# Linear attention into a SiLU layer on one core: units 12 to 15 join the seven-product scheme, half of the scores are masked in SBUF, and the last product ends in three pieces

## The chip, the cores and the metric

The kernel runs on one core of a Trainium2 chip. The metric is device time in microseconds (us) for one execution. The kernel before takes 203.23 us, the median of three runs (203.1, 203.23 and 203.87).

## What is computed

The reference first runs a blocked linear attention and then a two-layer network on its output (cut to what matters):

```python
# q, k, v: (4, 8, 768, 64) float32; lam: (8,); blocks of 64 positions
intra = (qb @ kb.T) * Dmask            # Dmask[i, j] = lam ** (i - j) where i >= j, else 0
out_b = intra @ vb + (qb * lam_pow) @ kv_state
kv_state = lam_block * kv_state + (kb * rev_pow).T @ vb
...
x = out.transpose(0, 2, 1, 3).reshape(3072, 512)
h = x @ w_in                           # 512 -> 2048
g = h * sigmoid(h)                     # SiLU
return g @ w_out                       # 2048 -> 512, float32
```

The decay `lam ** (i - j)` is split into a factor on v and a factor on the result, so the scores themselves are only multiplied by a triangle of ones and zeros.

## The kernel before, in words

**Units, pairs, groups.** The 3072 rows are cut into 24 units of 128 rows. Attention works on pairs of units (12 pairs, three per batch entry). The first product (x @ w_in, here called P1) works on groups: four groups of two units for units 0 to 7, then groups of four for units 8 to 23. The second product (g @ w_out, P2) works on one unit (`product2`, L970) for units 0 to 11 and on four units (`product2_of_four`, L1061) from unit 12 on (`SEVENS = 12`).

**Attention of a pair.** `prepare` (L523) loads k, q and v in float32 (L429), casts k and q to bf16 (tile `kq`), scales v (`vd`) and gets the transposes `kqT`: on TensorE for the first four pairs, by one DMA transpose on SyncE's queue (L590) from pair 4 on. From pair 3 on, `burst` (L600) issues on TensorE, as one block of 64-row matmuls, the scores (L667) and states (L656) of the new pair and the outputs (L623, L630) of the pair before it. `attention` (L728) then reads the four score banks of a pair (two halves g, two row halves h) in PSUM, multiplies each by the triangle `tri` and writes bf16 into `st`: four VectorE operations of 128x512 a pair, the line that the profile gives as L411. The next burst reads `st`. The outputs are multiplied by the decay into `xt` (also L411), the input of P1.

**P1.** `product1` (L919) fills a PSUM bank with matmuls (L933) and ScalarE writes SiLU of it into `g` (L949). In a group of four units one tile takes four 128x512 matmuls, 64 in all for the group. `product1_of_four` (L1212), used for units 16 to 19 and 20 to 23 (`FIRST_SEVENS = (16, 20)`), forms the same result as seven products of sums in place of eight: 28 matmuls of 128x256 (L1252) for each of four quarters j, 112 a group. It needs sums of quarters of w_in (`wsum`, eight half tiles, `sums_of_w_in`, L1197), four differences of x (`xsum`), and for each j three copies of a bank (`to u` into another bank, `u2` and `u3` into SBUF) and two additions (`h22`, `h12`, L1015), with four SiLUs (L1268).

**P2.** `product2_of_four` forms seven products, too (L1124): numbers 3, 4, 5, 1, 2, 7, 6 of the table `SEVEN`, and for the last four units 3, 4, 2, 1, 5, 7, 6. It accumulates in PSUM on top of copies: product 3 goes into bank A, A is copied into bank P (`to P`), product 4 is added on P, the negative of P is copied into B (`to B`), and so on; a product cannot start before the copy that it adds on. It needs sums of w_out (`bsum`, L1015 on VectorE or GpSimd, or a DMA copy L1048 and an accumulating DMA L1051 for the three in `BMOVED`) and sums of g (`asum`, likewise, or by the DMAs L1105 and L1111 for units 12 to 19). For the last four units the last product (6) goes unit by unit into two banks, is copied out by VectorE (first unit, L406) and ScalarE (second unit, L404) and stored by two queues (L962).

**Order.** Nothing runs in the order in which the code is read. Every step is a task with a key (its due time), the engines that may do it and their costs, its dependencies and its buffers. `Planner.order` (L107) replays all tasks by those numbers and writes down the order for every engine; the instructions are then issued in that order, and each engine keeps it. `SHIFT` moves keys by tag and `HOME` fixes an engine for a tag. `LATE` and `TLATE` are the extra us that the plan allows for the landing of a load and of a transpose from pair 4 on (both 4.0). TensorE's idle stretches before 19 us in the plan are filled with matmuls on ones (L1319).

Of the kernel before, what the change touches and what calls it, by code (L numbers as in the profile page):

```python
# [39 lines left out]
def names_of(tag):  # L40


    if not isinstance(tag, tuple):
        return tag, None, None
    kind, n = tag[:2]
    if kind in ("cast", "scale", "burst", "mask", "y", "xe", "xf", "xt"):
        whole = "pair", n
    elif kind in ("first", "silu", "x", "to u", "u2", "u3", "h12", "h22"):
        whole = "group", n
    elif kind in ("seven", "a", "a copy", "to P", "to B", "to R", "on R", "m3", "c11", "c12", "c21", "c22"):  # L50
        whole = "four", n
    else:
        whole = None
    return tag, tag[:2] if len(tag) > 2 else None, whole


class Planner:
# [7 lines left out]

    SHIFT = {('cast', 11, 1, 0): -0.5, ('cast', 5, 0, 1): 2, ('cast', 7, 1, 0): 7, ('cast o', 2, 0): -5, ('first', 2, 3): 1.5,
             ('first', 2, 5): 3, ('first', 2, 7): 1.75, ('first', 5): 3.25, ('first', 5, 10): 6.25, ('first', 5, 12): 6,
             ('first', 5, 13): 10.25, ('first', 5, 15): 7, ('first', 5, 8): 3, ('first', 6): 7, ('first', 6, 0, 5): -3.75,
             ('first', 6, 1, 2): -0.25, ('first', 6, 1, 5): 5.5, ('first', 6, 2, 1): 1.25, ('first', 6, 2, 2): 4,
             ('first', 6, 2, 3): 7, ('first', 6, 3, 4): 0.25, ('first', 6, 3, 7): 5.5, ('first', 7, 0, 7): 1.5,  # L70
             ('first', 7, 1, 2): -6.75, ('four', 20): 2.5, ('group', 5): -6, ('group', 6): 0.5, ('inter', 2, 0): 9.75,
             ('load w', 3, 1): -1.5, ('pair', 10): -7.25, ('pair', 4): 0.25, ('pair', 5): -6, ('pair', 7): -9, ('pair', 9): -8.5,
             ('result', 1): -0.5, ('scale', 3, 0): -1, ('scale', 8): -5.5, ('second', 0): 2.25, ('seven', 12, 1): 10.5,
             ('seven', 16): 13.25, ('seven', 16, 6): 5.25, ('seven', 20): 14, ('store', 9): -2, ('to u', 7, 1): 0.5,
             ('turn', 1, 0, 0): -4.75, ('turned', 1, 0, 1): 5, ('turned', 2): 8.25, ('xe', 0, 0, 1): 4.5, ('xe', 3, 0, 0): 1.5,
             ('xe', 9, 0, 0): -3, ('xf', 6): -1.5, ('y', 10, 0, 0): -3.5, ('y', 6): -2.5, ('y', 8, 0, 0): -2}
    HOME = {('a', 20, 2, 1): 'POOL', ('b', 4, 0): 'POOL', ('cast', 10, 1, 0): 'DVE', ('cast', 11, 0, 0): 'ACT',
            ('cast', 11, 0, 1): 'DVE', ('cast', 11, 1, 0): 'ACT', ('cast', 11, 1, 1): 'DVE', ('cast', 3, 0, 1): 'ACT',
            ('cast', 4, 0, 0): 'ACT', ('cast', 4, 0, 1): 'DVE', ('cast', 5, 0, 0): 'POOL', ('cast', 5, 1, 0): 'ACT',
            ('cast', 7, 1, 0): 'DVE', ('cast', 8, 0, 0): 'POOL', ('cast', 8, 1, 0): 'POOL', ('cast', 9, 0, 0): 'POOL',  # L80
            ('cast', 9, 1, 0): 'POOL', ('cast o', 2, 0): 'DVE', ('cast o', 3, 1): 'DVE', ('cast o', 3, 3): 'DVE',
            ('cast w', 1, 3): 'POOL', ('result', 1): 'ACT', ('scale', 10, 0): 'POOL', ('to P', 12): 'ACT', ('to u', 7, 1): 'ACT',
            ('turned', 0, 1, 0): 'ACT', ('turned', 2, 0, 0): 'DVE', ('turned', 2, 0, 1): 'ACT', ('u3', 6, 0): 'ACT',
            ('u3', 7, 2): 'DVE', ('w', 3, 0): 'POOL', ('x', 6, 4): 'POOL', ('x', 7, 2): 'POOL', ('xe', 4, 0, 0): 'DVE',
            ('xe', 6, 0, 0): 'POOL'}
    FIRST, LAST, AHEAD = {"SP": 1.15, "ACT": 1.15, "POOL": 1.0}, 1.0, 0.75
# [196 lines left out]
def kernel(  # L283
# [130 lines left out]
    raw = {}  # L414
    LATE, TLATE = 4.0, 4.0

# [56 lines left out]

    groups = [[0, 1], [2, 3], [4, 5], [6, 7], ] + [list(range(4 * n, 4 * n + 4)) for n in range(2, NU // 4)]
    group_of = {u: (gi, i) for gi, us in enumerate(groups) for i, u in enumerate(us)}
# [252 lines left out]
    def attention(n):  # L728
# [332 lines left out]
    def product2_of_four(us):  # L1061
# [15 lines left out]
        def product(i, m, bank, opens, after=(), split=False):  # L1077
# [39 lines left out]
            prev, done = None, []  # L1117
            for p in ([(0,), (1,)] if split else [(0, 1)]):
                for ko in range(8):
                    buf, ready, lhs = left[ko]  # L1120

                    def mm(e, p=p, ko=ko, lhs=lhs):
                        for u in p:
                            nc.tensor.matmul(part(bank, u), lhsT=lhs(u), rhs=b_of(ko), stop=ko == 7, skip_group_check=True,  # L1124
                                             start=opens and not ko and not u)

                    prev = add((key + (ko + 8 * p[0] / len(p)) / 28, 2), {"PE": len(p) * (256 / 2400 + 0.0025)}, mm,
                               deps=[ready, bdeps[ko], prev] + list(after), kind="p2", tag=("seven", us[0], m),
# [51 lines left out]
        if not final:  # L1180
# [3 lines left out]
            return  # L1184
        for u, on, to in ((0, {"DVE": 0.42}, "SP"), (1, {"ACT": 0.39}, "ACT")):
            o = Buf("rawh")
            c22 = add(at(7), on, lambda e, u=u, o=o: copy(e, osb_of(o, 1)[:, 0], part(R, u)), deps=[m6[u]], bufs=[R[u], o], tag=("c22", tag, u))
            stored((at(7.3)[0], 7), halves_of[1], slice(128 * us[2 + u], 128 * us[2 + u] + 128), o, c22, on=to)

# [153 lines left out]
    at = 0.0  # L1343
# [40 lines left out]
```

## Time and profile before

| | before |
|---|---|
| runs | 203.1, 203.23, 203.87 us (median 203.23) |
| the profiled execution | 203.53 us, of which its span is 201.6 us and 1.93 us lie around it |
| mean granted TensorE clock | 0.999 |
| P1, units 8 to 15: matmuls 128x512 (L933) | 128 |
| P1 by seven products: matmuls 128x256 (L1252) | 224 |
| VectorE busy, 100 to 120 us, its fullest stretch of 20 us | 17.25 of 20 us |
| HBM read and written | 27.27 and 6.29 MB |

How to read it: the span runs from the first to the last instruction of the profiled execution. The page names engines PE (TensorE), PEld (its weight loads), DVE (VectorE), ACT (ScalarE), POOL (GpSimd) and SP (SyncE); a q behind the name is the queue that issues DMAs. In a group of instructions, "out<-in xcount | busy, mean ns | idle before <-releaser" gives what is written from what, how many, the total in us, the mean duration of one in ns, and how long the engine had been idle just ahead of them and for whom. The chain of work that ended last lists, in order of time, start in us, duration in us and what ran. A matmul's own duration reaches beyond the start of the next one, so the pace of a row of matmuls is read from that chain (duration over count), not from the mean.

### The profile page before, as it was taken

Reading aid. Unit: us, or ns where it says so; the run is one execution under the profiler, and the core shown is the slowest. Engines: PE = TensorE matmul, PEld = TensorE weight load, DVE = VectorE, ACT = ScalarE, POOL = GpSimd, SP = SyncE. Lnnn points to the kernel's source line nnn. Section 1 sums busy time; section 2 is a strip of 40 time slices with the busy share of each in tenths; the row PEclk is TensorE's granted clock in tenths of the full one; section 3 lists DMA queues with packets and bytes.
Section 4 is the critical chain, followed back from the end, with each engine's and each line's share of the span. In section 5 each row is a group of like instructions: output and inputs, shape, how many; then the busy total and the mean of one; then the engine's idle time right before and its main releaser. Section 6 shows DMA issues by size and latency. Waiting matters only on the chain.

```text
span 201.6 us, 5956 instructions
## 1 busy us (share of the span) xinstructions
PE 195.3 (97%) x2526; PEld 138.2 (69%) x2526; DVE 142.3 (71%) x235; ACT 122.3 (61%) x189; POOL 68.2 (34%) x81
## 2 busy tenths in 40 slices
PE   6998999999999999999999999999999999999993
PEld 2776788867766554544545455458888888888882
DVE  3798848686972649599596987983854758837282
ACT  3776798838786533178777515756775688862210
POOL 4024510524602020589053305418862433004000
PEclk9999999999999999999999999999999999999999
DMA  4999999999999999989999999938998969002223
GB/s 109 331 343 367 368 366 345 379 295 378 287 210 291 249 336 337 319 216 278 268 223 324 222 259 215 183 105 181 188 176 245 193 226 196 9 3 104 81 99 135
DMA packets 77898, 47.57 MB, mean 236 GB/s; under 512 B 18544, under 2 KB 70768, under 8 KB 77872
## 3 DMA queue, kind: packets, MB, share of 16 engines
q1 hardware_dynamic: 64976, 35.79, 64.4%
q0 software_dynamic: 8576, 6.03, 20.8%
q10 hardware_dynamic: 4320, 5.38, 7.4%
q8 instruction: 20, 0.33, 0.6%
q14 instruction: 6, 0.05, 0.1%
HBM read 27.27 MB, written 6.29 MB: 166 GB/s over the span
## 4 chain that ended last, share of the span: by engine, by line
PE 89%; SPq 5%; DMA 3%; ACT 1%; issue 0%
PE banks L933 28%; PE banks L975 21%; PE banks L1124 18%; PE banks L1252 12%; SPq L429 4%; DMA raw_w<-in_moe_w_in_dram 3%; PE banks L667 2%; PE banks L623 2%; PE banks L630 1%; PE banks L656 1%; PE banks L575 1%; SPq L448 1%; PE banks L896 1%; PE banks L846 1%; PE banks L877 0%
## 5 line engine op out<-in xcount | busy, mean ns | idle before, releaser
L933 PE MATMUL banks<-xt,w_in_bf 128*128 128x256 bf16 (+1 forms) x384 | 64.2, 308 | 0.7 <-ACT w_in_bf L404 0.4
L949 ACT ACTIVATE g<-banks 128x512 bf16<-128x512 f32 x64 | 46.3, 744 | 18.5 <-PE banks L933 15.7
L933 PEld LDWEIGHTS <-w_in_bf 128*128 128x128 bf16 x384 | 36.7, 98 | 20.4 <-ACT w_in_bf L404 0.6
L975 PE MATMUL banks<-w_out_bf,g 128*128 128x512 bf16 x192 | 47.7, 379 | 0.0
L411 DVE TENSOR_TENSOR st<-banks,tri 128x512 bf16<-128x512 f32 (+1 forms) x42 | 29.9, 759 | 5.8 <-PE banks L667 4.2
L975 PEld LDWEIGHTS <-g 128*128 128x128 bf16 x192 | 18.2, 98 | 19.8
L411 DVE TENSOR_TENSOR xt<-banks,lam_xe 128x512 bf16<-128x512 f32 x24 | 16.0, 687 | 13.3 <-PE banks L623 9.7
L404 ACT ACTIVATE osb<-banks 128x512 f32<-128x512 f32 (+1 forms) x15 | 8.7, 581 | 24.1 <-PE banks L975 18.4
L408 POOL CAST kq<-raw 64x512 bf16<-64x512 f32 (+1 forms) x16 | 15.0, 961 | 18.1 <-DMA raw<-in_q_dram 16.1
L404 ACT ACTIVATE kq<-raw 64x1024 bf16<-64x1024 f32 (+2 forms) x21 | 18.1, 883 | 2.5 <-DMA raw<-in_v_dram 1.5
L1124 PE MATMUL banks<-bsum,g 128*128 128x256 bf16 x160 | 19.4, 273 | 0.0
L1124 PEld LDWEIGHTS <-asum 128*128 128x128 bf16 x176 | 17.2, 98 | 2.0
L1124 PEld LDWEIGHTS <-g 128*128 128x128 bf16 x160 | 15.7, 98 | 1.8
L1111 POOL DMA_DIRECT2D asum<-g x8 | 9.9, 1281 | 17.8 <-DMA asum<-g 11.0
L411 DVE TENSOR_TENSOR vd<-raw,lam_v 128x1024 bf16<-128x1024 f32 (+1 forms) x12 | 13.6, 1130 | 3.0 <-DMA raw<-in_v_dram 2.9
L1268 ACT ACTIVATE g<-banks 128x512 bf16<-128x512 f32 x16 | 11.6, 741 | 4.5 <-PE banks L1252 4.3
L1252 PE MATMUL banks<-xsum,wsum 128*128 128x256 bf16 x96 | 14.2, 273 | 0.0
L1252 PEld LDWEIGHTS <-wsum 128*128 128x128 bf16 x128 | 12.4, 98 | 1.7
L411 POOL TENSOR_TENSOR xf<-y,lam_be 128x256 f32<-128x256 f32 (+1 forms) x6 | 4.9, 811 | 22.9 <-DVE y L787 16.9
L1319 PE MATMUL banks<-ones 128*128 128x128 bf16 (+1 forms) x90 | 10.9, 271 | 1.5 <-DVE ones L355 1.5
L1015 DVE TENSOR_TENSOR tmp<-banks,tmp 128x512 f32<-128x512 f32 x16 | 10.9, 688 | 2.0 <-ACT tmp L404 1.1
L406 DVE CAST kq<-raw 64x512 bf16<-64x512 f32 (+3 forms) x21 | 10.3, 512 | 2.9 <-DMA raw<-in_k_dram 2.5
(96 smaller groups left out, 284.4 us busy)
## 6 DMA issues: line engine op xcount, KB each, us to landing
raw<-in_k_dram SPq DMA_DIRECT2D x11, 512.0 KB, 7.3
raw<-in_q_dram SPq DMA_DIRECT2D x11, 512.0 KB, 6.0
raw<-in_v_dram SPq DMA_DIRECT2D x11, 512.0 KB, 6.7
out_dram<-osb ACTq DMA_DIRECT2D x20, 256.0 KB, 4.4
raw_w<-in_moe_w_in_dram SPq DMA_DIRECT2D x8, 512.0 KB, 7.9
raw_w<-in_moe_w_out_dram SPq DMA_DIRECT2D x8, 512.0 KB, 7.0
asum<-g SPq DMA_DIRECT2D x8, 256.0 KB, 2.6
asum<-g POOLq DMA_DIRECT2D x8, 256.0 KB, 5.3
```

Of the source, the lines that this page charges most:

```text
L404: nc.scalar.activation(o, i, AF.Copy)
L406: nc.vector.tensor_copy(o, i)
L408: nc.gpsimd.tensor_copy(o, i)
L411: (nc.vector if e == "DVE" else nc.gpsimd).tensor_tensor(o, a, b, op=AL.mult)
L933: nc.tensor.matmul(t[:, j, :], lhsT=w_in_bf[:, ko, 128 * m:128 * m + 128], rhs=xt[gi].tile[:, ko, :], start=(ko == 0), stop=(ko == KI - 1))
L949: nc.scalar.activation(t.rearrange("p j (c a r) -> p (j c) r a", c=n // U, r=2), psum_of(bank).rearrange("p (jc r a) -> p jc r a", r=2, a= ...
L975: nc.tensor.matmul(psum_of(bank), lhsT=gs[gi, ko][1](1, 128 * gp, 128)[:, 0], rhs=w_out_bf[:, ko], start=(ko == 0), stop=(ko == KO - 1))
L1015: (nc.vector if e == "DVE" else nc.gpsimd).tensor_tensor(o, x, y, op=op)
L1124: nc.tensor.matmul(part(bank, u), lhsT=lhs(u), rhs=b_of(ko), stop=ko == 7, skip_group_check=True, start=opens and not ko and not u)
L1252: nc.tensor.matmul(two_of(bank)[:, f], lhsT=(wb[0].tile if wb else w_quarter(*wl))[:, ko, fs], rhs=(xsum(xr) if isinstance(xr, int) else x ...
L1268: nc.scalar.activation(t.rearrange("p j (c a r) -> p (j c) r a", c=2, r=2), src().rearrange("p (jc r a) -> p jc r a", r=2, a=64), AF.Silu)
L1319: nc.tensor.matmul((t if b.pool == "bank" else t[:, 0])[:, 0:w], lhsT=ones[:, 0:128], rhs=ones[:, 0:w], start=True, stop=True)
```

## The change

The edit has four parts beside a new set of `SHIFT` and `HOME` entries.

1. `FIRST_SEVENS` gains 12: the group of units 12 to 15 goes through `product1_of_four`. The sums of w_in are now needed for this group as well, so earlier.
2. For pairs 4 to 11 and row half h = 1 (two of the four score banks of a pair), ScalarE copies the bank to `st` as bf16 (tag `take`), and VectorE or GpSimd then multiplies `st` in place by a bf16 triangle `tri_bf` (tag `mask`). The other two banks are masked from PSUM as before.
3. The last product of the last four units is issued as unit 0 with 256 columns, then unit 1 with columns 0 to 127, then unit 1 with columns 128 to 255, each copied and stored by itself.
4. `BMOVED` is emptied: the three sums of w_out that DMAs formed are formed by VectorE or GpSimd. `POOLED` becomes (6, 7): two results are stored by GpSimd's queue. `LATE` and `TLATE` go from 4.0 to 1.0, so the plan lets casts, transposes and bursts stand earlier against TensorE's work.

```diff
-    SHIFT = {('cast', 11, 1, 0): -0.5, ('cast', 5, 0, 1): 2, ...
+    SHIFT = {('a', 12, 6, 1): 10.25, ('a', 20, 6, 1): -9.75, ('b', 6): 7, ...
-    HOME = {('a', 20, 2, 1): 'POOL', ('b', 4, 0): 'POOL', ...
+    HOME = {('a', 12, 1, 1): 'POOL', ('a', 20, 1, 1): 'POOL', ...
...
+    TAKEN = range(4, 12), (1,)
-    BMOVED, POOLED = (1, 7, 6), (6,)
+    BMOVED, POOLED = (), (6, 7)
-    TKEY, SEVENS, LAG, WSKEY, FIRST_SEVENS = 9.0, 12, 5.0, 14.0, (16, 20)
+    TKEY, SEVENS, LAG, WSKEY, FIRST_SEVENS = 9.0, 12, 5.0, 14.0, (12, 16, 20)
...
-    LATE, TLATE = 4.0, 4.0
+    LATE, TLATE = 1.0, 1.0
...
+                    if n in TAKEN[0] and h in TAKEN[1]:
+                        def take(e, st=st, b=b, h=h):
+                            copy(e, tile_of(st, [128, 4, 4 * 64], BF16, "st")[:, 2 * h:2 * h + 2, :], psum_of(b).rearrange("p (m s) -> p m s", m=2))
+
+                        def erase(e, st=st, h=h):
+                            t = st.tile[:, 2 * h:2 * h + 2, :]
+                            mult(e, t, t, tri_bf.rearrange("p r q a -> p (r q a)")[:, None, :].to_broadcast([128, 2, 256]))
+
+                        t = add((s - 0.9, 0, g, h), {"ACT": 0.6}, take, deps=[bursts[1 + g]], bufs=[b, st], tag=("take", n, g, h))
+                        masked.append(add((s - 0.85, 0, g, h), {"DVE": 0.42, "POOL": 1.6}, erase, deps=[t, tri_done], bufs=[st], tag=("mask", n, g, h), lock=True))
+                        continue
...
-            for p in ([(0,), (1,)] if split else [(0, 1)]):
+            for i, (p, cs) in enumerate([((0,), slice(0, 256)), ((1,), slice(0, 128)), ((1,), slice(128, 256))] if split
+                                        else [((0, 1), slice(0, 256))]):
...
-                            nc.tensor.matmul(part(bank, u), lhsT=lhs(u), rhs=b_of(ko), stop=ko == 7, skip_group_check=True,
+                            nc.tensor.matmul(part(bank, u)[:, cs], lhsT=lhs(u), rhs=b_of(ko)[:, cs], stop=ko == 7, skip_group_check=True,
...
-        for u, on, to in ((0, {"DVE": 0.42}, "SP"), (1, {"ACT": 0.39}, "ACT")):
+        for i, (u, cs, on, to) in enumerate(((0, slice(0, 256), {"DVE": 0.42}, "SP"), (1, slice(0, 128), {"DVE": 0.29}, "SP"),
+                                             (1, slice(128, 256), {"ACT": 0.28}, "ACT"))):
...
+    tri_bf = const.tile([128, 2, 2, 64], BF16, name="tri_bf")
+    tri_done = add((-2.9, 0), {"POOL": 0.5}, lambda e: nc.gpsimd.tensor_copy(tri_bf, tri), tag="tri")
```

More of the change, by code (lines that the diff above doesn't have):

```diff
@@ L45, in names_of @@
     kind, n = tag[:2]
-    if kind in ("cast", "scale", "burst", "mask", "y", "xe", "xf", "xt"):
+    if kind in ("cast", "scale", "burst", "mask", "take", "y", "xe", "xf", "xt"):
         whole = "pair", n
@@ L64 @@
     SWITCH = 0.095
[L66 to L85, printed above, removed]
+    SHIFT = {('a', 12, 6, 1): 10.25, ('a', 20, 6, 1): -9.75, ('b', 6): 7, ('cast', 11, 1, 0): -4, ('cast', 11, 1, 1): -0.25,
+             ('cast', 4): 9, ('cast', 4, 0, 0): 0.25, ('cast', 6): -4, ('cast', 8, 1, 0): -4, ('cast', 9, 0, 0): 3.5,
+             ('cast o', 1, 2): 0.25, ('cast o', 2): 5.75, ('first', 2): -11.75, ('first', 2, 1): -5.25, ('first', 2, 6): -11.25,
+             ('first', 3): -0.5, ('first', 3, 5): 2, ('first', 5, 1, 5): 2, ('first', 5, 3, 5): 6.25, ('first', 6): -2.75,
+             ('first', 6, 2, 5): -2.5, ('first', 6, 3, 4): 5.75, ('first', 7): -2.25, ('first', 7, 1, 3): 11.75,
+             ('four', 12): -2.75, ('four', 16): 9.75, ('group', 2): 4.75, ('group', 3): 0.75, ('group', 4): -3.75,
+             ('group', 5): -11.25, ('group', 6): -4, ('group', 7): 0.5, ('load w', 3, 1): -1.5, ('mask', 11, 0, 1): 3,
+             ('mask', 4): 9.5, ('mask', 5): 2.25, ('mask', 5, 1, 0): -1.5, ('mask', 5, 1, 1): -3, ('mask', 6): -3.5,
+             ('mask', 6, 0, 1): 3, ('mask', 7): 0.25, ('mask', 8, 1, 0): -11.25, ('outputs', 1, 1): -9.25, ('outputs', 2, 0): 13.75,
+             ('pair', 10): 9, ('pair', 11): 11.75, ('pair', 4): -7.75, ('pair', 7): -5.75, ('pair', 8): 1.5, ('pair', 9): 1.5,
+             ('scale', 3, 0): -1, ('second', 0): 3.25, ('second', 1): -10.25, ('second', 6): 0.5, ('seven', 12): -4.5,
+             ('seven', 12, 2): 3.75, ('seven', 12, 7): 9.5, ('silu', 5): 3, ('silu', 5, 3, 1, 1): 2.5, ('states', 2, 0): 12.5,
+             ('x', 6): -4, ('x', 6, 1): 5, ('x', 7, 1): 10.5, ('xe', 0, 0, 1): 4.5, ('xe', 3, 0, 0): 1.5, ('xf', 9): 2.75,
+             ('xt', 5): -9, ('y', 10): -2, ('y', 10, 0, 0): -9.25, ('y', 11): 2, ('y', 5): 1.5}
@@ L471 @@
             load_w(n - 100, x[0], int(x[1:]))
-    groups = [[0, 1], [2, 3], [4, 5], [6, 7], ] + [list(range(4 * n, 4 * n + 4)) for n in range(2, NU // 4)]
+    groups = [[0, 1], [2, 3], [4, 5], [6, 7]] + [list(range(4 * n, 4 * n + 4)) for n in range(2, NU // 4)]
     group_of = {u: (gi, i) for gi, us in enumerate(groups) for i, u in enumerate(us)}
@@ L1184, in product2_of_four, with last @@
             return
-        for u, on, to in ((0, {"DVE": 0.42}, "SP"), (1, {"ACT": 0.39}, "ACT")):
+        for i, (u, cs, on, to) in enumerate(((0, slice(0, 256), {"DVE": 0.42}, "SP"), (1, slice(0, 128), {"DVE": 0.29}, "SP"),
+                                             (1, slice(128, 256), {"ACT": 0.28}, "ACT"))):
             o = Buf("rawh")
-            c22 = add(at(7), on, lambda e, u=u, o=o: copy(e, osb_of(o, 1)[:, 0], part(R, u)), deps=[m6[u]], bufs=[R[u], o], tag=("c22", tag, u))
-            stored((at(7.3)[0], 7), halves_of[1], slice(128 * us[2 + u], 128 * us[2 + u] + 128), o, c22, on=to)
+            def last(e, u=u, o=o, cs=cs):
+                copy(e, tile_of(o, [128, 1, cs.stop - cs.start], F32, "osb")[:, 0], part(R, u)[:, cs])
+            c22 = add(at(7), on, last, deps=[m6[i]], bufs=[R[u], o], tag=("c22", tag, i))
+            stored((at(7.3)[0], 7), slice(256 + cs.start, 256 + cs.stop), slice(128 * us[2 + u], 128 * us[2 + u] + 128), o, c22, on=to)
     wsum = {}
```

13 lines of the change are left out of this document (11 added, 2 removed), and 3 rows, old and new, of the table HOME.

## The prediction

> **What bounds the kernel now.** I read the page's busy shares first, then who TensorE waits for, then the chain of work that ended last, in order of time. The first line is the page's busy time, then come the two longest lines of TensorE's waits, apart from one for the ones of the warm-up: what waited, for what, us in total, how often, longest.
>
> ```profile
> PE 195.3 (97%) x2526; PEld 138.2 (69%) x2526; DVE 142.3 (71%) x235; ACT 122.3 (61%) x189; POOL 68.2 (34%) x81
> ```
>
> ```profile
> PE banks L933 <- ACT w_in_bf L404: 0.4, 1, 0.4
> PE banks L933 <- POOL w_in_bf L408: 0.4, 1, 0.4
> ```
>
> A share of 97% could still be slow work, so the chain matters more (start, duration, what ran):
>
> ```profile
> 17.49 0.64 ACT w_in_bf L404
> 18.17 0.83 PE banks L933 x6
> ...
> 27.39 0.45 PE banks L575 x8
> ...
> 69.08 5.18 PE banks L975 x24
> ...
> 159.96 4.15 PE banks L1252 x38
> ...
> 175.90 22.29 PE banks L1124 x204
> 198.20 0.38 ACT osb L404
> ```
>
> From 18.17 to 198.2 us nothing but TensorE carries the chain, and at an even pace: 5.18/24 = 216 ns for 512 columns, 4.15/38 and 22.29/204 = 109 ns for 256, 0.45/8 = 56 ns for 128. So the time is three things: 18.2 us until w_in is cast, 180 us of TensorE's columns, 3.4 us from the last matmul to the end. Fewer columns shorten it one for one; work on other engines costs nothing until TensorE stands still for it. Before has next to no standing still to lose, so every new one adds.
>
> **The change, part by part.** All sums are against the profiled execution, 203.53 us (span 201.6, 1.93 around it); it lies 0.30 above the median 203.23, so I add the sum to the median.
>
> 1. *Units 12 to 15.* Removed: 64 matmuls of 512 columns, 64 x 0.216 = 13.82 us. Added: 112 of 256, 112 x 0.109 = 12.23 us. **-1.59 us**, all of it on the path.
>
> 2. *A new gap ahead of units 16 to 19's second P2 product.* In the changed order the burst of pair 11 no longer follows units 12 to 15's P1 but stands 26 us of TensorE work later, and behind it TensorE has only P2 of units 16 to 19 to do: product 3 (16 matmuls) and then at once product 4, which adds on the copy `to P` of product 3. Nothing stands between. In before each such copy has other matmuls beside it. The price, from these rows (groups of instructions, shapes apart; then the end of the run, in order of time):
>
> ```profile
> L411 DVE TENSOR_TENSOR st<-banks,tri 128x512 bf16<-128x512 f32 x36 | 22.6, 682 | 4.2 <-PE banks L667 4.2
> ...
> L1015 DVE TENSOR_TENSOR wsum<-w_in_bf 128x1024 bf16<-128x1024 bf16 x3 | 5.1, 1737 | 0.0
> ...
> L404 ACT ACTIVATE banks<-banks 128x512 f32<-128x512 f32 x8 | 4.7, 598 | 4.9 <-PE banks L1124 2.9 <-PE banks L1252 2.0
> L1015 POOL TENSOR_TENSOR xsum<-xt,xsum 128x512 bf16<-128x512 bf16 x2 | 4.7, 2346 | 0.0
> ...
> L1015 DVE TENSOR_TENSOR xsum<-xt,xsum 128x512 bf16<-128x512 bf16 x2 | 0.8, 417 | 0.0
> ```
>
> ```profile
> 197.33 0.43 DVE L406 COPY osb<-banks 128x256 f32<-128x256 f32 x1
> ...
> 198.20 0.38 ACT L404 ACTIVATE osb<-banks 128x256 f32<-128x256 f32 x1 [2.90 <-PE banks L1124]
> ```
>
> The last matmul starts at 197.90, ScalarE's copy of its bank at 198.20: 0.30. The copy takes 0.60, and TensorE follows ScalarE by 0.04 (17.49 + 0.64 = 18.13, then 18.17). 0.30 + 0.60 + 0.04 - 0.11 (the last matmul's own slot) = **+0.83 us**; 0.75 to 1.4, the upper end if ScalarE is still on the second `take` of pair 11. Behind that wait on TensorE stand the outputs of pair 11 and, behind them, all P1 of units 20 to 23, so it is lost whole. The next copy, `to B`, is covered by that burst.
>
> 3. *Product 3 of units 12 to 15 waits for all SiLUs of the group.* Between the last `u3` copy and it, ScalarE has that copy and six SiLUs, 0.2 + 0.60 + 6 x 0.75 = 5.3 us; TensorE has 16 matmuls of 256 columns, nine of 512 and a burst (130.35 to 132.15 less one slot: 1.6), together 5.3 us. **+0.1 us** (0 to 0.4).
>
> 4. *The new end.* The last unit's 8 x 109 ns become 16 x 56 ns: +0.02. But its two pieces lie in one PSUM bank. In the changed order VectorE's copy of the first piece waits for TensorE's 13th of those 16 matmuls, and the 14th waits for that copy. Copies take 0.43 for 256 columns and 0.69 for 512, so 0.29 for 128; ahead of it 0.30 as above less 0.05 for the shorter matmul, behind it 0.04, less a slot of 0.06: a gap of +0.53. ScalarE's last copy is shorter (0.38 for 256 columns, 0.60 for 512: 0.28 for 128), -0.10, and the last matmul and store are shorter by 0.05 to 0.1. **+0.38 us** (-0.1, if the copy overlapped, to +0.5). The row speaks of banks only through these waits. [...]
>
> 5. *Masks in SBUF.* Each pair loses two VectorE rows of 682 ns and gains two ScalarE copies (595 ns, the row of a copy out of PSUM) and two bf16 products. These are not in the trace; bounds are 417 ns (the bf16 row above) and 682, on VectorE, 1.06 us (half of a 128x1024 GpSimd row of 2.1) and 2.35 on GpSimd, which has four of them. I take 417 and 1.6. VectorE: 16 x 0.68 = 10.9 us become 12 x 0.42 = 5.0; ScalarE gains 16 x 0.60 = 9.6.
>
> 6. *Load of the engines.* Units 12 to 15 bring 12 bank copies, 8 additions of 0.69 and 4 differences; six halves of w_out sums come from DMAs to VectorE and GpSimd, and more results are copied by VectorE (8 of 12, before 1). By counts of the new order times these rows VectorE goes from 142 to about 153 us, ScalarE from 122 to about 132. Cover: before's fullest 20 us have VectorE busy for 17.25 with TensorE never idle, and queued masks start every 0.60 us while each takes 0.68. I take **0** (0 to +1.6).
>
> 7. *Loads and transposes.* The bursts of pairs 4 to 8 stand 4.7, 4.0, 4.4, 6.4 and 4.0 us of TensorE work earlier. In before they start at 66.1, 74.0, 82.9, 96.6 and 107.5 and their transposes land at 60.5, 70.4, 77.4, 88.6 and 97.6. With these landings unchanged four clear by 0.9 us or more, and pair 5 is 0.4 late; but the new order issues the transposes of pairs 4 to 6 one load sooner, worth 1.5 us (the loads of pair 5 land at 53.6, 55.1 and 56.6). **0** (0 to +2.4).
>
> 8. *The start.* TensorE waits twice 0.4 us for w_in casts and fills the rest with ones. The new order has one score block ahead of the second wait (0.35 and two switches of 0.1), and three P1 matmuls behind it (0.33). **0** (-0.9 to +0.5).
>
> Sum: -1.59 + 0.83 + 0.10 + 0.38 = **-0.28**, so 203.25 for the profiled execution and **203.0 us** for the median, its own range 202.3 to 203.7. About 0.5%, 1.0 us here, is what a measurement of this kernel can tell from no change, so this is "same".
>
> **Rivals.**
>
> - *The start gives something* (201.9): if both waits for w_in go and the score is done in their time, -0.9 comes to the sum. For it: TensorE's waits there are real. Against: the loads' order is the same, and w_in's second part lands at 17.46 in either. It also covers the case that gap 2 is partly filled.
> - *Slower: transposes late* (204.9). The bursts of pairs 4 to 6 have slack of about 1 to 2.6 us by step 7. Should the landings come 2 us later than in before, pair 4 waits 62.5 - 61.4 = 1.1, and pair 5, pushed on by it, 72.4 - 71.1 = 1.3, in all 2.4 - 0.28 = +2.1, less a part that other stalls would have had: +1.7. It decides from 1 us of lateness on. For it: a landing takes 6.0 to 9.7 us from issue and DMAs are nine tenths busy until 70 us. Against: fewer loads stand ahead.
> - *Slower: VectorE and GpSimd in each other's way* (204.3). The row of `wsum` at 1737 ns beside others at 688 and 886 and GpSimd's 2346 show bf16 work in SBUF losing 1 us when both are at it. The moved masks are of this kind, and in the stretch of units 12 to 15 every copy is waited for. Two losses of 0.8 us ahead of a burst give -0.28 + 1.6 = +1.3. It decides when VectorE falls over 0.6 us behind. [...]
> - *The mask is no cheaper in SBUF*: at 682 ns VectorE has 12 x 0.27 = 3.2 us more over 100 us; part of the rival before.
>
> **How the numbers follow.** Forecast 0.50; start 0.13; transposes 0.17; VectorE and GpSimd 0.20. Range 201.9 to 205.0: it takes in the rivals' values and leaves out the rest of their tails. Faster by over 0.5% (under 202.2): 0.14, the start and a little of the forecast. Within 0.5%: 0.54, the forecast and a third of the last rival. Slower: 0.32.
>
> **What would show it.** 112 more matmuls of the seven-product line at 109 ns and 64 fewer of 512 columns; a TensorE gap of 0.8 us for ScalarE's `banks` copy near 160 us; one of 0.5 us for VectorE's `osb` copy just before the end; no wait over 0.4 us elsewhere. Waits for `kqT` near 61, 70 or 78 us would prove the second rival, waits for VectorE's `tmp`, `st` or `xt` between 80 and 140 us the third. A first P1 matmul at its steady pace before 17.5 us would prove the first.

## The result, and the profile after

The changed kernel takes 205.36 us, the median of 22 runs (203.6 to 211.48), and the kernel before 203.53 us in 22 runs beside it: ratio 1.0061, 95% interval 1.004 to 1.0083, so slower by about 0.6%. The predicted 203.0 us and the upper end of the range, 205.0, are both passed. Ratios here leave out executions over 1.5% above the fastest of their kernel, medians do not, and of the profiles of shift140, masks_on_vector and fewer_ones, which were of that kind, no size of a gap is used.

The profiled execution took 204.29 us, of which 202.6 are its span. First the page's busy times of the kernel after, then TensorE's waits (us in total, times, longest; that of the warm-up and three of 0.2 and 0.3 us left out).

```profile
PE 193.7 (96%) x2568; PEld 142.9 (71%) x2581; DVE 155.5 (77%) x259; ACT 130.9 (65%) x201; POOL 71.8 (35%) x91
```

```profile
PE banks L1144 <- issue: 0.9, 1, 0.9
PE banks L994 <- issue: 0.8, 5, 0.2
PE banks L1144 <- ACT banks L412: 0.7, 1, 0.7
PE banks L1144 <- DVE osb L414: 0.4, 1, 0.4
```

Line numbers are those of the new file: L952 is P1, L1277 P1 by seven products, L994 P2, L1144 P2 by seven, L412 and L414 the copies of ScalarE and VectorE, L419 the multiplication. The third and fourth lines are the predicted waits, for `to P` and for the copy in the new end. The first was not predicted: TensorE stood still and the trace knows nothing it waited for. The second is none: 13 of the 192 matmuls of L994 have no record (192 weight loads have), and five times the hole comes right behind a burst and so counts as idle time.

The chain of work that ended last, in order of time (start, duration, what ran), at the five places where TensorE stood still:

```profile
85.39 7.27 DMA raw<-in_q_dram
92.68 1.06 ACT kq L412
93.73 0.49 ACT st L412
94.27 8.79 PE banks L952 x40
...
125.17 0.41 DVE st L419
125.58 0.61 DVE tmp L414
126.23 2.12 PE banks L1277 x18
...
133.10 1.20 PE banks L1144 x10
134.30 0.91 issue
135.21 0.82 PE banks L1144 x6
...
160.24 1.87 PE banks L1144 x16
162.18 0.59 ACT banks L412
162.81 1.91 PE banks L1144 x16
...
199.05 0.30 DVE osb L414
199.40 0.34 PE banks L1144 x3
```

In the chain of before TensorE carries everything from 18.17 us to the last copy; here it hands over five times. Read from the starts of the matmuls (start to start, less one slot), the gaps are 0.40, 0.28, 1.07, 0.87 and 0.54 us. The last two are steps 2 and 4 (0.83 and 0.53 predicted). The first three, 1.75 us, are not in the sum. At 92.7 us ScalarE's in-order queue is in the way: the cast of pair 9's q waits for a load that lands at 92.66, and behind it stands the `take` of pair 7 that sets a PSUM bank free for P1.

What the same program does in another execution (run again, below) tells most about them. All in us; the end of the span is read from the trace to 0.01 us:

| | before | after | after, second profile | shift8 |
|---|---|---|---|---|
| columns of units 12 to 15 | 0 | -1.59 | -1.59 | -1.59 |
| gap at 92 to 95 | 0 | 0.40 | 0 | 1.44 |
| gap at 125 to 127 | 0 | 0.28 | 0.07 | 0.24 |
| gap in product 3 of units 12 to 15 (134) | 0 | 1.07 | 0 | 0 |
| gap at 140 to 142 | 0 | 0 | 0 | 0.67 |
| gap for `to P` (160 to 163) | 0 | 0.87 | 0.88 | 0.87 |
| gap in the new end | 0 | 0.54 | 0.54 | 0.54 |
| last matmul's start to the end of the span | 3.70 | 3.05 | 3.05 | 3.04 |
| around the span | 1.93 | 1.73 | 1.71 | 1.73 |
| execution | 203.53 | 204.29 | 202.65 | 204.98 |

The rows add up to 0.72 of 0.76 us in after, -0.97 of -0.88 in the second profile, and 1.31 of 1.45 in shift8 (the same program but for eight warm-up instructions). Put the other way: the second profile's 202.65 us and the gaps that it lacks give 204.33 for after (204.29 measured) and 204.93 for shift8 (204.98).

### The profile page after: what moved, and what is told of

Its sections match the earlier page's. It is cut to its first block, busy times and chain, and to the rows that moved or that the text cites. A ratio compares the mean times of both kernels' runs of the same rounds, so it can differ in the third digit from the quotient of the medians.

```text
span 202.6 us, 6099 instructions
## 1 busy us (share of the span) xinstructions
PE 193.7 (96%) x2568; PEld 142.9 (71%) x2581; DVE 155.5 (77%) x259; ACT 130.9 (65%) x201; POOL 71.8 (35%) x91
## 4 chain that ended last, share of the span: by engine, by line
PE 79%; DMA 7%; SPq 6%; DVE 2%; ACT 2%; issue 2%; POOL 1%; ACTq 0%; POOLq 0%
PE banks L1144 19%; PE banks L952 18%; PE banks L1277 17%; PE banks L994 16%; SPq L437 4%; DMA raw<-in_q_dram 4%; DMA raw_w<-in_moe_w_in_dram 3%; PE banks L631 2%; PE banks L675 2%; DVE st L419 1%; PE banks L638 1%; SPq L598 1%; PE banks L664 1%; PE banks L583 1%; SPq L456 1%
## 5 line engine op out<-in xcount | busy, mean ns | idle before, releaser
L952 PE MATMUL banks<-xt,w_in_bf 128*128 128x256 bf16 (+1 forms) x320 | 48.5, 294 | 0.6 <-ACT w_in_bf L412 0.3
L994 PE MATMUL banks<-w_out_bf,g 128*128 128x512 bf16 x179 | 46.1, 379 | 1.2 <-issue 0.8
L952 PEld LDWEIGHTS <-w_in_bf 128*128 128x128 bf16 x320 | 30.6, 98 | 14.5 <-ACT w_in_bf L412 0.6
L968 ACT ACTIVATE g<-banks 128x512 bf16<-128x512 f32 x48 | 34.2, 740 | 8.0 <-PE banks L952 6.6
L994 PEld LDWEIGHTS <-g 128*128 128x128 bf16 x192 | 18.1, 98 | 16.9
L412 ACT ACTIVATE kq<-raw 64x1024 bf16<-64x1024 f32 (+3 forms) x26 | 23.0, 899 | 4.4 <-DMA raw<-in_k_dram 2.1
L1144 PE MATMUL banks<-bsum,g 128*128 128x256 bf16 x160 | 21.2, 273 | 1.6 <-issue 0.9
L419 DVE TENSOR_TENSOR xt<-banks,lam_xe 128x512 bf16<-128x512 f32 x24 | 15.9, 685 | 7.7 <-PE banks L631 4.1
L419 DVE TENSOR_TENSOR st<-banks,tri 128x512 bf16<-128x512 f32 (+1 forms) x26 | 20.3, 805 | 1.6 <-PE banks L675 0.8
L1277 PEld LDWEIGHTS <-wsum 128*128 128x128 bf16 x192 | 18.8, 98 | 3.3 <-issue 0.3
L1293 ACT ACTIVATE g<-banks 128x512 bf16<-128x512 f32 x24 | 17.5, 739 | 5.6 <-PE banks L1277 3.6
L1277 PE MATMUL banks<-xsum,wsum 128*128 128x256 bf16 x144 | 20.3, 272 | 0.1
L1293 ACT ACTIVATE g<-tmp 128x512 bf16<-128x512 f32 x24 | 17.7, 768 | 3.8 <-DVE tmp L1034 3.7
L1144 PEld LDWEIGHTS <-asum 128*128 128x128 bf16 x184 | 17.4, 98 | 2.5 <-issue 0.5
L1144 PEld LDWEIGHTS <-g 128*128 128x128 bf16 x160 | 15.5, 98 | 3.9 <-issue 2.0
L419 DVE TENSOR_TENSOR vd<-raw,lam_v 128x1024 bf16<-128x1024 f32 (+1 forms) x12 | 13.6, 1131 | 4.4 <-DMA raw<-in_v_dram 4.3
L1034 POOL TENSOR_TENSOR asum<-g 128x1024 bf16<-128x1024 bf16 x5 | 11.2, 2257 | 14.8 <-ACT g L1293 9.6
L414 DVE CAST kq<-raw 64x512 bf16<-64x512 f32 (+3 forms) x21 | 11.7, 591 | 6.1 <-DMA raw<-in_k_dram 3.8
L1277 PEld LDWEIGHTS <-w_in_bf 128*128 128x128 bf16 x144 | 14.1, 98 | 2.8
L412 ACT ACTIVATE st<-banks 128x512 bf16<-128x512 f32 x16 | 8.7, 592 | 11.3 <-PE banks L675 11.3
```

What stands on the lines that cost most here:

```text
L412: nc.scalar.activation(o, i, AF.Copy)
L414: nc.vector.tensor_copy(o, i)
L419: (nc.vector if e == "DVE" else nc.gpsimd).tensor_tensor(o, a, b, op=AL.mult)
L952: nc.tensor.matmul(t[:, j, :], lhsT=w_in_bf[:, ko, 128 * m:128 * m + 128], rhs=xt[gi].tile[:, ko, :], start=(ko == 0), stop=(ko == KI - 1))
L968: nc.scalar.activation(t.rearrange("p j (c a r) -> p (j c) r a", c=n // U, r=2), psum_of(bank).rearrange("p (jc r a) -> p jc r a", r=2, a= ...
L994: nc.tensor.matmul(psum_of(bank), lhsT=gs[gi, ko][1](1, 128 * gp, 128)[:, 0], rhs=w_out_bf[:, ko], start=(ko == 0), stop=(ko == KO - 1))
```

## The experiments

| run | median of all, us | ratio to before, 95% interval |
|---|---|---|
| again (the changed kernel) | 205.91 | 1.0037 (0.9985 to 1.0089) |
| shift8 | 204.97 | 1.0073 (1.005 to 1.0097) |
| shift140 | 206.58 | 1.0083 (1.0042 to 1.0124) |
| fewer_ones | 205.92 | 1.0041 (0.9995 to 1.0086) |
| before_shift140 | 205.6 | 1.0111 (1.0081 to 1.014) |
| old_end | 204.09 | 0.9982 (0.9943 to 1.0021) |
| before_new_end | 204.96 | 1.0066 (1.004 to 1.0093) |
| before_new_end_fewer | 204.5 | 1.0028 (1.0003 to 1.0053) |
| cast9_behind | 203.93 | 1.0003 (0.9966 to 1.004) |
| casts_behind | 205.08 | 1.0065 (1.0038 to 1.0093) |
| casts_behind_2 | 204.36 | 1.0015 (0.9984 to 1.0046) |
| masks_on_vector | 209.49 | 1.0146 (1.0087 to 1.0205) |
| casts_and_mask10 | 203.64 | 0.9997 (0.996 to 1.0034) |
| combined | 204.47 | 1.0018 (0.998 to 1.0055) |
| best | 203.75 | 0.9997 (0.9957 to 1.0037) |
| best_2 | 203.45 | 1.0004 (0.9974 to 1.0033) |

The kernel before had medians of 203.44 to 204.05 us beside them. The changed kernel itself gave 1.0061 and 1.0037, and 33 of its 34 executions lie between 202.65 and 207.18 us (the other took 211.48); differences between two runs of under 0.4% say little here, so the traces carry most verdicts.

### The same kernel again

> The changed kernel itself once more, as the reference for the two runs beside it and for what a second profile of it shows. Late loads and VectorE beside GpSimd should show again: a gap of 0.4 to 1.5 us at 92 to 95 us and 0.2 to 0.7 us at 125 to 126 and at 137 to 142 us; a block of instructions that comes late at 3779 may or may not. Time 204.2 to 205.4.

The profiled execution took 202.65 us, the fastest of its 12, and TensorE's waits in it are these, all of them:

```profile
PE banks L1346 <- DVE ones L363: 1.5, 1, 1.5
PE banks L994 <- issue: 0.8, 5, 0.2
PE banks L1144 <- ACT banks L412: 0.7, 1, 0.7
PE banks L1144 <- DVE osb L414: 0.4, 1, 0.4
PE banks L952 <- ACT w_in_bf L412: 0.2, 1, 0.2
PE banks L631 <- PE banks L638: 0.2, 1, 0.2
```

The expected gaps did not show: apart from 0.07 us at 125.7, only the two predicted ones are there. So the other three are no fixed part of the program, but differ between executions of it. Pair 9's q landed at 90.27 us here and at 92.66 in the first profile. Yet most executions are not like this one: 25 of the 34 of the changed kernel are over 204.78 us. This fastest execution is 0.88 us below the profiled one of before, but only 0.33 below the fastest one of before (202.98), so undisturbed the change gives some 0.3 to 0.9 us.

### Late loads

First what ScalarE and VectorE waited for loads of q, k and v between 40 and 140 us; before has one such line, the other four are those of after:

```profile
ACT kq L404 <- DMA raw<-in_v_dram: 1.5, 1, 1.5
...
ACT kq L412 <- DMA raw<-in_q_dram: 1.3, 1, 1.3
ACT kq L412 <- DMA raw<-in_k_dram: 1.1, 2, 0.9
DVE vd L419 <- DMA raw<-in_v_dram: 2.1, 3, 1.1
DVE kq L414 <- DMA raw<-in_k_dram: 1.2, 1, 1.2
```

cast9_behind, then casts_behind and casts_behind_2, move tasks in the finished order and leave all else as it is. In `behind(a, b)`, whose definition is left out here, a is issued next after b on its engine.

```diff
 planned = plan.order()
+behind(('cast', 9, 0, 0), ('take', 7, 1, 1))
+behind(('cast', 9, 0, 1), ('cast', 9, 0, 0))
```

> The changed kernel with ScalarE's two casts of pair 9 moved behind its two takes of pair 7; nothing else moves. Theory 'late loads' (a cast that waits for its load stands in ScalarE's queue ahead of the take that frees a bank for P1): the TensorE gap of 0.4 us near 93.6 us goes, and the time falls by 0.3 to 0.4 us in the profile and by more in the slower executions. Rival: pair 9 is then late itself (its transpose lands later and its burst waits) and the time stays or rises.

Measured: the gap stayed, 0.40 us at 92.7, now behind VectorE's `xt`. ScalarE was only half of it. The profiled execution, 203.94 us, fits its gaps (0.40, 0.29 and 0.65, 1.34 in all, for 1.75 in after). The ratio fell to 1.0003 and the median to 203.93, though two causes are still there; that stays unexplained.

VectorE's half is plain in the chain of shift8, whose gap was 1.44 us:

```profile
83.55 8.54 DMA raw<-in_k_dram
...
92.45 0.43 DVE kq L414
92.90 0.69 DVE wsum L1034
93.59 0.61 DVE xt L419
94.25 1.24 PE banks L994 x5
```

Pair 9's k lands at 92.09, 8.5 us after its issue. VectorE's cast of it waits, the `xt` of pair 6 stands two operations behind, and TensorE needs the bank that `xt` reads.

```diff
+behind(('scale', 8, 0), ('xt', 6, 0))
+behind(('cast', 9, 1, 0), ('scale', 8, 0))
```

> The changed kernel with the casts that wait for late loads moved back in both queues: ScalarE's two casts of pair 9 behind its takes of pair 7, VectorE's scaling of v of pair 8 and its cast of pair 9 behind the first xt of pair 6; nothing else moves. Theory 'late loads': the TensorE gap at 92 to 95 us (0.40, 1.44, 0.48 and 0.40 us in the four profiles so far) falls under 0.15 us, and the time falls by 0.4 to 0.9 us against the changed kernel (205.0). Rival: the transposes of pairs 8 and 9 land later and their bursts wait instead; the time stays.

Measured: no gain (1.0065). The casts now stood ahead of the masks of pair 7, whose banks P1 needs as well, and TensorE waited 1.15 us at 94.9 for one of those. My move was wrong, not the theory; casts_behind_2 puts them behind those too.

```diff
-behind(('scale', 8, 0), ('xt', 6, 0))
+behind(('scale', 8, 0), ('mask', 7, 1, 0))
```

> As casts_behind, but VectorE's scaling of v of pair 8 and its cast of pair 9 go behind its two masks of pair 7 out of PSUM as well (in casts_behind they stood ahead of them, and TensorE waited 1.15 us for the second mask's bank). Theory 'late loads': no TensorE gap over 0.15 us is left between 90 and 97 us, and the time falls by 0.4 to 1.0 us against the changed kernel (205.0). Rival: what is moved back is late for its own burst, and the time stays.

Measured: no gap between 90 and 97 us, none for the bursts of pairs 8 and 9, 1.0015, median 204.36 against 205.4 for the changed kernel (all its 34 executions). The interval, 0.9984 to 1.0046, still touches that of the changed kernel, so the gap is shown to go, and the fall of the time is likely. What was left in its profile, 0.58 and 0.23 us at 138, is the next cause.

### VectorE beside GpSimd

In the profile of casts_behind_2 (VectorE, then GpSimd; start, duration):

```profile
135.87 1.75 DVE L1034 TENSOR_TENSOR xsum<-xt 128x512 bf16<-128x512 bf16 x1
137.54 0.69 DVE L414 COPY banks<-banks 128x512 f32<-128x512 f32 x1
```

```profile
136.19 2.42 POOL L419 TENSOR_TENSOR st<-st,tri_bf 128x512 bf16<-128x512 bf16 x1
```

A VectorE addition of two tiles in SBUF takes 1.75 us beside GpSimd's mask of pair 10 (2.39 in shift8, 2.36 in cast9_behind), and 0.41 alone. The copy out of PSUM beside the same mask takes its usual 0.69. It is the third rival, and at 125 us it shows once more: two of the new masks on VectorE take 1.84 us in place of 0.8 while GpSimd scales v of pair 11 (1.90 us). First after, then the second profile of the same program:

```profile
123.06 1.90 POOL L419 TENSOR_TENSOR vd<-raw,lam_v 128x1024 bf16<-128x1024 f32 x1 [0.72 <-DMA raw<-in_v_dram]
123.74 1.84 DVE L419 TENSOR_TENSOR st<-st,tri_bf 128x512 bf16<-128x512 bf16 x2
...
122.52 1.90 POOL L419 TENSOR_TENSOR vd<-raw,lam_v 128x1024 bf16<-128x1024 f32 x1 [0.50 <-DMA raw<-in_v_dram]
123.42 1.62 DVE L419 TENSOR_TENSOR st<-st,tri_bf 128x512 bf16<-128x512 bf16 x2
```

GpSimd starts when v lands. The later it starts against the masks, the longer they take, and TensorE's gap behind them grows by as much: masks of 1.62, 1.74, 1.84 and 1.93 us go with gaps of 0.07, 0.19, 0.28 and 0.38 us (again, casts_and_mask10, after, best).

What in the hardware makes it so, no run shows.

```diff
+planned[:] = [(s, i, 'DVE' if e == 'POOL' and t.tag and t.tag[0] == 'mask' else e, t) for s, i, e, t in planned]
```

> The changed kernel with the four masks of GpSimd (pairs 4, 6, 10 and 11) given to VectorE in the same places; nothing else moves. Theory 'VectorE and GpSimd in each other's way' (the third rival as predicted): the xsum that took 2.4 us beside GpSimd's mask of pair 10 takes 0.42, the TensorE gap of 0.65 us near 140 us goes, and the time falls by 0.3 to 0.7 us against the changed kernel (205.0). Rival 'VectorE is the bound': its queue is four masks of 0.42 us longer, and the time stays or rises by up to 0.4 us.

Measured: inconclusive; the ratio, 1.0146, rests on three executions, with an interval of 1.0087 to 1.0205. casts_and_mask10 asks the same of the one mask that collided, on top of casts_behind_2:

```diff
+planned[:] = [(s, i, 'DVE' if t.tag == ('mask', 10, 0, 1) else e, t) for s, i, e, t in planned]
```

> casts_behind_2 with GpSimd's mask of pair 10 given to VectorE in the same place. In casts_behind_2 the xsum beside that mask took 1.75 us in place of 0.41 and TensorE stood still for 0.58 and 0.23 us behind it. Theory 'VectorE and GpSimd in each other's way': all four xsum take 0.41, no gap over 0.15 us is left between 134 and 143 us, and the time falls by 0.3 to 0.8 us against casts_behind_2 (204.4) and by 1 us or more against the changed kernel. Rival 'VectorE is the bound': one more operation in its queue costs what the collision did, and the time stays.

Measured: all four `xsum` take 0.41 or 0.42, one of them this:

```profile
136.14 0.41 DVE L1034 TENSOR_TENSOR xsum<-xt 128x512 bf16<-128x512 bf16 x1
```

No gap is left between 134 and 143 us, though GpSimd issues the same four DMAs in that time. The ratio is 0.9997, the median 203.64, and all 12 executions lie between 203.03 and 204.78. The fall against casts_behind_2 (0.7 us by the medians) is inside the intervals; against the changed kernel it is 1.8 us by the medians, and the interval lies below that of its first 22 runs, though not below the wide one of again.

Two smaller gaps are left, 0.19 us at 126 and 0.27 at 97.5. The second is a late load again, now in GpSimd's queue:

```profile
86.86 7.42 DMA raw<-in_q_dram
...
95.72 0.81 POOL kq L416
96.61 0.67 POOL xf L419
97.31 0.44 DVE y L795
```

The cast of q waits for its load, `xf` stands behind it on GpSimd, VectorE's `y` needs `xf`, and TensorE goes on when `y` is done.

### The block of instructions that comes late

The page counts the packets that carry instructions; q8 is TensorE's, by the size:

```profile
q8 instruction: 20, 0.33, 0.7%
```

That is 16 KB a packet. TensorE has 5,173 recorded instructions, and 13 matmuls without a record; 0.33 MB for these is 64 bytes for each, so a packet holds 256 of them. In after, the gap lies ahead of instruction 3779 of TensorE's stream. No wait of the program stands there.

```diff
-occupy(vacant(0.5, start), FIRST_ONES, 512)
+b = vacant(0.5, start); occupy(b, 9, 512); occupy(b, 5, 102)
```

> The changed kernel with the tenth warm-up matmul on ones (512 columns) cut into five of 102: four more matmuls, eight more instructions in TensorE's stream, no change anywhere else. In the changed kernel TensorE stands still for 1.08 us after the tenth of the 16 matmuls of units 12 to 15's product 3, and no semaphore wait stands there. Theory 'instructions late' (TensorE's stream comes in blocks of 256 instructions and the block that begins there arrives late): the gap moves with the count, to after the sixth matmul of product 3, with 0.5 to 2 us; the time stays that of the changed kernel (204.3 to 205.4). Rival 'data late' (the weights in g or the port they are read through): the gap stays behind the tenth matmul.

Measured: no gap in product 3 at all, so it said nothing of the place; it showed the other gaps instead.

```diff
-occupy(vacant(0.5, start), FIRST_ONES, 512)
+b = vacant(0.5, start); occupy(b, 80, 64)
```

> The changed kernel with the ten warm-up matmuls on ones cut into 80 of 64 columns: the same columns, 140 more instructions ahead of everything else. Theory 'instructions late': the block that came late inside product 3 now begins inside the burst of pair 10 and is asked for some 4 us earlier, so product 3 of units 12 to 15 runs at 109 ns throughout and the time falls by 0.8 to 1.2 us against the changed kernel. Rival 'data late': the gap behind the tenth matmul stays and the time is that of the changed kernel.

Measured: no gap in product 3, but a new one at 18.6 us, ahead of instruction 707, again with nothing that it waited for; slower on the whole. 707 and 3779 differ by 3072, which is 12 x 256. Other runs stood still at 3779 as well. In before_new_end it is the only such line among TensorE's waits:

```profile
PE banks L623 <- issue: 0.8, 1, 0.8
```

| profile | instruction after the gap | gap, us | packet of q8 ends | TensorE goes on |
|---|---|---|---|---|
| after | 3779 | 1.07 | 133.61 | 135.21 |
| before_new_end | 3779 | 0.99 | 131.21 | 132.50 |
| best | 3779 | 0.50 | 132.81 | 134.27 |
| masks_on_vector | 3779 | (size not used) | 138.91 | 140.19 |
| shift140 | 707 | (size not used) | 19.93 | 21.24 |
| after, second profile | 3779, no gap | 0 | 131.81 | 133.59 |

Five gaps at a boundary between blocks of 256, four of them at the same one, and each ends 1.28 to 1.60 us behind a packet's end. In all 18 profiles the packets and these boundaries go one to one, and TensorE never enters a block less than 1.28 us behind the end of its packet. So that the block came late is shown.

Why it is this block can be read, too. TensorE of the changed kernel gets through the 256 instructions ahead of 3779 in 4.75 us where nothing stops it, faster than through any other block; in before they take 6.90. In the second profile the packet starts 1.98 us into that time and takes 0.98 us, which is just soon enough; in after it starts at 2.37 and takes 1.86. Why a packet starts late or takes long is not shown; in before_new_end it starts at 5.68, late enough for a gap there as well.

Most blocks come in time: of 20 crossings from one block to the next in after, one stops TensorE, for 1.07 us.

```diff
-occupy(vacant(0.5, start), FIRST_ONES, 512)
+b = vacant(0.5, start); occupy(b, 80, 64)
```

> The kernel before with its ten warm-up matmuls on ones cut into 80 of 64 columns: the same columns, 140 more instructions in TensorE's stream, no other change. The same edit of the changed kernel left TensorE standing still for 2.5 us at instruction 707 of its stream, with no wait there, and 707 + 12 x 256 = 3779 is where the changed kernel stood still for 1.07 us. Theory 'instructions late': this edit does the same here, a gap of 0.5 to 3 us between 17 and 21 us at instruction 707 that the trace can put down to nothing, and the time rises by 0.5 to 2.5 us over the kernel before. Rival (the gap belongs to the changed kernel's data or order): the time is that of the kernel before within 0.5 us.

Measured: 1.0111, slower by 2.0 us by the medians, as expected, but for another reason. The trace puts the gap, at instruction 702, down to the cast of w_in, whose load was issued at 11.94 and landed at 19.31, in place of 10.72 and 17.46; the first packet of instructions went out at 8.55 us, among the first loads, not at 12.64. So 140 more instructions cost 2 us here, but not in the way the theory had it. That the early packet is what delayed the load is not shown.

```diff
-occupy(b, int((start - at) / 0.056 * 0.75), 128)
+occupy(b, int((start - at) / 0.056 * 0.75 / 4 + 0.5), 512)
```

> The changed kernel with the matmuls on ones that fill TensorE's idle stretches before 19 us made of 512 columns in place of 128, a quarter as many: 116 instructions fewer in TensorE's stream, nothing else moves. Theory 'instructions late': the block that began at instruction 3779, which stood still there for 1.04 to 4.47 us in three of the profiles so far, now begins 116 instructions later in the work, past the burst of pair 10 and product 3 of units 12 to 15. So no gap over 0.3 us that the trace puts down to nothing is left between 126 and 141 us, and if the typical execution has that gap the time falls by 0.5 to 1.1 us against the changed kernel (205.0). Rival: the gap is rare, and the time stays within 0.3 us.

Measured: no such gap between 126 and 141 us, yet no gain either (1.0041, median 205.92). Undecided. In the two other runs that carry this edit, combined and before_new_end_fewer, TensorE's wait for ScalarE's cast of w_in is 0.66 and 0.96 us, against 0.35 to 0.54 with the warm-up as it was, so it costs at the start what it may save later.

### The new end

```diff
-for i, (p, cs) in enumerate([((0,), slice(0, 256)), ((1,), slice(0, 128)), ((1,), slice(128, 256))] if split
+for i, (p, cs) in enumerate([((0,), slice(0, 256)), ((1,), slice(0, 256))] if split
```

(and the copies and stores likewise.)

> The changed kernel with the end of the kernel before: the last product in two pieces of one unit each, all else in the same order. By step 4 as predicted (the new end costs 0.38 us) the time falls by 0.4 us. By the account of the two profiles (a gap of 0.55 in, but 0.6 less from the last matmul to the end) it stays within 0.15 us.

Measured: the gap of 0.54 goes, the last matmul's start to the end takes 3.46 in place of 3.05: 0.15 us by the trace. The ratio fell by far more, to 0.9982, though the profile still has the gaps at 95 us (0.48) and 127 us (0.37) and two waits for w_out (0.53 and 0.41). That fall stays unexplained; best and casts_and_mask10 differ by the same edit and not in time.

before_new_end is the opposite edit of the kernel before, the diff of the change alone.

> The kernel before with the new end of the run alone: last product in three pieces, the order is otherwise the same. Step 4 as predicted: 0.38 us slower. By the account of the profiles (0.54 of gap and 0.02 of shorter matmuls against 0.40 less from the last matmul to the end): 0.16 us slower. Rival, that the shorter last copy and store win: 0.1 us faster.

Measured: 1.0066. Its profile (204.99) has 0.54 and 0.02 in and 0.28 out at the end (3.42 for 3.70), 0.28 in all, and 0.99 at instruction 3779. In this kernel and in before that instruction lies inside the burst of pair 10; before has no gap there.

> The kernel before with the new end and with the warm-up of fewer_ones (118 instructions fewer). The new end alone took 1.3 us more than the kernel before, of which its profile shows 0.54 of gap at the end less 0.33 of shorter tail, and 0.99 of standing still at instruction 3779. Theory 'instructions late': here that gap goes, and the time is 0.1 to 0.5 us above the kernel before. Rival, that the new end itself costs 1.3 us: it stays 1.0 us or more above.

(The diff is that of fewer_ones.) Measured: the gap at 3779 is gone, 1.0028, between the two theories: 0.57 us above before, of which 0.28 at the end and 0.4 for w_in at the start by the profile. So the end costs 0.15 to 0.3 us.

### Put together

combined is casts_and_mask10 with the old end and the warm-up of fewer_ones; best is it without the latter; best_2 shortens only the longest filling of the warm-up, by 32 instructions.

> The changed kernel with fewer_ones, casts_behind_2, the old end, and GpSimd's mask of pair 10 given to VectorE. By the account of the gaps (0.5 to 1.1 for instructions, 0.4 to 1.0 for late loads, 0.16 for the end, up to 0.65 for the mask) it takes 202.5 to 203.5 us and is at least as fast as the kernel before (203.6). Rival: the gaps come back elsewhere, and it stays above 204.3.

> casts_and_mask10 with the old end. By the account of the gaps it is 0.16 us faster than casts_and_mask10, and by the sum (1.59 us of columns, 0.87 for the copy to P, 0.3 at 125 us) 0.3 to 0.8 us faster than the kernel before. Rival, if the new end costs more than its gap: 0.5 us or more faster than casts_and_mask10.

> best with the longest filling of the warm-up (22 matmuls of 128 columns on ones) made of six of 512: 32 instructions fewer in TensorE's stream. In best the block at instruction 3779 came late again, 0.50 us in the profile. Theory 'instructions late': the block now begins 32 instructions further on in the work, some 2 us later, and no gap that the trace puts down to nothing is left between 126 and 141 us; the time falls by 0.2 to 0.5 us against best (203.75) and is at or under that of the kernel before (203.5). Rival: other late blocks or the start take it back, and it stays.

Measured: 1.0018, 0.9997 and 1.0004. combined lost 0.66 us to w_in at the start and 0.53 to w_out. best and best_2 are as fast as the kernel before, not faster; their profiles (203.11 and 202.79) keep the 0.87 for `to P`, 0.3 to 0.4 at 125 us and, in best alone, 0.50 at instruction 3779; best_2 has 0.30 at 82.5, behind an `xt` of VectorE. No version is faster than the kernel before by what can be measured.

## Why the prediction was wrong

1. *Units 12 to 15*, -1.59: right (1.31 us for 12 matmuls, 109 ns).
2. *Gap for `to P`*, +0.83: right; 0.87 to 0.88 in every profile of it.
3. *Product 3 and the SiLUs*, +0.1: no wait for them there.
4. *The new end*, +0.38: the gap was right (0.54 for 0.53), the shorter tail was mis-sized (0.28 to 0.41 for 0.15 to 0.2); 0.15 to 0.3 in all. The changed kernel's end is shorter by another 0.24 us that old_end has, too (3.46 for 3.70), and 0.2 us less lie around its span; the prediction has neither, and no run says where they come from.
5. *Masks in SBUF*: right when alone (0.41 on VectorE for 0.417; 1.33 on GpSimd for 1.6; 592 ns for ScalarE's copy).
6. *Load of the engines*, "I take **0**": **this step failed, too.** The loads were right (155.5 and 130.9 us for 153 and 132), the price was not. The third rival came true in part, in after with 0.28 us and in shift8 with 0.91, where it was priced at 1.6. Its sign, a wait for VectorE's `tmp`, `st` or `xt`, could not tell it from step 7: the `xt` of shift8 was held up by a load.
7. *Loads and transposes*, "**0**": **the step that failed first.** It asked whether transposes land before their bursts. They did, in every profile but those of masks_on_vector and fewer_ones. What came late were casts that wait for loads, in VectorE's and ScalarE's queues ahead of work that frees PSUM: 0.40 to 1.44 us of TensorE. Between 40 and 140 us these two waited 5.7 us for loads of q, k and v in after and 9.1 in shift8, and 1.5 in before. How long they wait is not the price: in casts_and_mask10 these casts and scalings still wait 4.7 us, and TensorE stands still for none of them.
8. *The start*, 0: right; the first steady P1 at 17.88 for 18.17.

A late block of instructions was in no step: 1.07 us in the profiled execution, the largest single miss there.

The sum comes near where none of this happens (202.65 in the second profile, 203.25 predicted for an execution), but in part by luck: `to P`, the columns and the gap in the end are right to 0.1 us, while the shorter end and the time around the span give 0.87 us where the sum has 0.15 to 0.2. Each rival alone stayed inside the range; that several gaps come in one execution was not reckoned with, and so the median passed its upper end. Two of the rivals' values do not follow from their own sums: -0.9 in 203.23 - 0.28 gives 202.05 and not 201.9, and +1.6 gives 204.55 and not 204.3.

That the gaps of steps 6 and 7 come from late loads and from VectorE beside GpSimd is shown: in traces of several kernels, and by casts_behind_2 and casts_and_mask10, where the gaps go with the order. With three cast tasks of pair 9, one scaling and one mask moved, the 0.6% are gone. What share each cause has in the typical execution is not shown: old_end and cast9_behind leave the causes in place and are as fast, and how often a block of instructions is late is known for the profiled executions alone.

## What to carry to other kernels

When loads are let closer to their use, the deadline of the last consumer is not the price: look down each in-order queue for what stands behind the operation that waits, above all for what frees a PSUM bank (0.40 to 1.44 us of TensorE here). The masks that were moved from PSUM to SBUF were slowed by GpSimd's work (two of them took VectorE 1.62 to 1.93 us in place of 0.8), and a copy out of PSUM kept its 0.69; so such an operand is priced with the row beside GpSimd, not with the row alone. A stretch of short matmuls uses up instructions fast (256 in 4.75 us in after, where before takes 6.90); look whether the next block of them can be there in time. Take a second profile of the same program before explaining the first: here 204.29 and 202.65 us were one kernel.

## What was not expected of the hardware

TensorE's instructions came by DMA in packets of 16 KB, 256 to a packet by the count above, and a block that came late left it standing still for 0.50 to 1.07 us with no wait in the program; in four of the five gaps it was the block at 3779, which in after stands behind the fastest 256 instructions (4.75 us). Eighty matmuls of 64 columns at the start of before_shift140 took 4.45 us, as ten of 512 do in before, so there columns alone set the time. Two bf16 masks in SBUF took 1.62 to 1.93 us on VectorE in place of 0.8 beside one scaling of 1.90 us on GpSimd.
